# The second weight matrix's scale taken at the first second-product step, and the square of v written into the v tile

## The chip, the cores and the metric

The kernel runs on one core of a Trainium2 chip. Its time is the device time of one execution in microseconds (us); three executions were timed, and their median counts. TensorE (PE) does the matrix products, VectorE (DVE), ScalarE (ACT) and GpSimd (POOL) the rest, and SyncE (SP) starts most of the transfers. Each engine works through its own queue in order.

## The reference, cut to what matters

```python
# attention: B, H, S, D = 4, 8, 576, 64, fp32
scores = causal(q @ k.T / 8 + min(-(cum_i - cum_j), 0))   # cum = cumsum(max(s, 0))
x = softmax(scores) @ v                                    # heads joined: [4, 576, 512]
# first layer
u  = x + real(fft(fft(x, axis=1), axis=2))
un = (u - mean(u)) / sqrt(var(u) + 1e-6)
x  = u + relu(un @ moe_w_ch1) @ moe_w_ch2                  # 512 -> 2048 -> 512
# second layer: the same normalisation (times g_ln) and MLP, without the FFT
```

The weights come as 64-bit floats.

## The kernel before

**Work and stages.** The four batches go through attention, the Fourier layer, a normalisation and the first MLP one after another, in such a way that the MLP of one batch runs beside the attention and the Fourier layer of the next. The second MLP of all batches follows at the end. Attention is worked in pairs of heads, four pairs for a batch: pairs 0 to 3 are batch 0, pairs 4 to 7 batch 1. For these two batches q and k stay in fp32: `prep_pair32` transposes them on TensorE (`tp`, L974 to L985), then come the scores (`s`, L1031), their reduction on VectorE (L1037), the exponentials on ScalarE (L773, L774), a product with the other factor of the decay (`p`, L784), a transpose of `p` by a DMA (`pT`, L788 and L796) and the product with v (`pv`, L818).

**Fourier layer.** `fft_steps` adds and subtracts the two halves of the tokens and of the features into the tiles `eo` (fp16 high and low halves, L1119 and L1120, three tiles for a batch), multiplies by the token matrix (`y`, L1138, 36 products), takes one column apart (`ps`, L1159), and multiplies by the feature matrix (`z`, L1179, 36 products). `emit_ln` normalises the result: `u` (L344, L347), whose tiles a DMA of SP's queue transposes to `unT` (L348).

**Products in two halves.** Except for q and k of batches 0 and 1, each operand of a product is scaled by a power of two and split into a high and a low fp16 half; three products replace one. The scale comes from a norm: squares are summed by ScalarE along with the Square activation, added over the partitions by a small product with ones (`total`, L82, on TensorE) and turned into a power of two by a few operations of one column on VectorE (`pow2_scale`, L93 to L98).

**Weights of the first MLP.** `wa` holds 32 blocks: 0 to 15 of the first matrix, 16 to 31 of the second. `prep` loads each block (512 KB), converts it from 64 bits to fp32 with three VectorE operations (L150, L153, L156; they read the staging tiles `xset` or `wide`), squares it on ScalarE (L167) and splits it on ScalarE (L194) and VectorE (L195). `scale(0)` takes the scale of the first matrix, `scale(1)` that of the second: `wtot` (L171), `total`, and `c2` (L183), by which the second product is multiplied at the end. While `late` is set, the second matrix is split block by block in `emit_g2`, two blocks for each second-product step `m` of batch 0's first chunk.

**MLP.** A chunk is two tiles of 128 tokens; `emit_g1` makes the first product (`g<-unT,wa`, L373) with its rectifier (`h`, L379, L380), and `emit_g2` the second (L395).

**What sets the order.** The kernel is written as generators that are stepped in turn, and a list scheduler then orders the instructions of each engine by a simulated timeline, with priorities. A tile of a pool with `bufs=2` that is asked for a third time waits until the first is free. The square of a pair's v (L991) writes results that nobody reads, into a junk tile of the tag `u16`, which it shares with the `u` tiles and with the weights' squares. The tile for the split v has the tag `v16`.

Of the kernel before, what the change touches and what calls it, by code (L numbers as in the profile page):

```python
# [8 lines left out]
F16 = mybir.dt.float16  # L9
BF16 = mybir.dt.bfloat16  # L10
I32 = mybir.dt.int32
AF = mybir.ActivationFunctionType
# [21 lines left out]
def fused_kernel(ctx: ExitStack, tc, q, k, v, s, wa1, wa2, g_ln, wb1, wb2, tok_c, feat_c, ident_c, rev_c, bias_c, out):  # L34
# [5 lines left out]
    mpool = ctx.enter_context(tc.tile_pool(name="mpool", bufs=2))  # L40
# [7 lines left out]
    att = att_stack.enter_context(tc.tile_pool(name="att", bufs=1))  # L48
# [29 lines left out]
    def total(parts):  # L78

        n = parts.shape[1]  # L80
        ps = ps_s.tile([128, 512], F32, tag="s", name="total")[:, 0:n]
        nc.tensor.matmul(out=ps, lhsT=ones.to_broadcast([128, 128]), rhs=parts, start=True, stop=True)  # L82
        res = small.tile([128, n], F32, tag=f"total{n}", name="total")
        nc.vector.tensor_copy(out=res, in_=ps)
        return res
# [16 lines left out]
    class Weights:  # L102
# [110 lines left out]
        def prep(self):  # L213

            for i in range(len(self.wide + self.extra)):
                self.load(i)
                yield KN["COST"][0]
            held = []
            for i in range(16):
                self.convert(i)  # L220
                self.square(i)
                again = [n for n in range(i + 1, 32) if self.PLACE[n] == self.PLACE[i]]
                if again and self.HOLD and again[0] >= 16:
                    held.append(again[0])
                elif again:
                    self.load(again[0])
                yield KN["COST"][1]
            self.scale(0)
            yield KN["COST"][2]
            left = self.left = list(range(16))  # L230
            for _ in range(KN["S1"] if self.HOLD else KN["S1B"]):
                self.split(left.pop(0))
                yield KN["COST"][3]
            for n, i in enumerate(held):
                self.load(i)
                if n % KN["HOLDN"] == KN["HOLDN"] - 1 or n == len(held) - 1:
                    yield 1.0
            for i in range(16, 32):
                self.convert(i)
                self.square(i)  # L240
                again = [n for n in range(i + 1, 32) if self.PLACE[n] == self.PLACE[i]]
                if again:
                    self.load(again[0])
                yield KN["COST"][1]
                for _ in range(KN["S2"]):
                    if left:
                        self.split(left.pop(0))
                        yield KN["COST"][3]
            while len(left) > (KN["LAZY"] if self.late else 0):
                self.split(left.pop(0))  # L250
                yield KN["COST"][3]
            self.scale(1)
            yield KN["COST"][2]
            for i in range(self.LAST if not self.late else 0):
                self.split(16 + i)
                yield KN["COST"][4]
# [127 lines left out]

    def emit_g2(ch, m, h):
        if m == 0:
            nc.gpsimd.tensor_tensor(out=ch.f, in0=ch.f, in1=ch.w.c2.to_broadcast([128, 2]), op=ALU.mult)
            ch.ps = [ps_2.tile([128, 512], F32, tag=f"g2{j}", name=f"g2{j}") for j in range(2)]
        for i in range(2):
            if ch.w.late:  # L390
                ch.w.split(16 + m + i)
            for j in range(2):
                c = 256 * i + 128 * j
                for n, (lh, lw) in enumerate(((0, 0), (0, 1), (1, 0))):
                    nc.tensor.matmul(  # L395
                        out=ch.ps[j], lhsT=h[:, lh, c:c + 128], rhs=ch.w.w2(lw, m + i),
                        start=(m + i + n == 0), stop=(m + i == MB - 1 and n == 2),
                    )
        if m == MB - 2:
            ch.w.late = False  # L400
            for j in range(2):
                o = mpool.tile([128, 512], F32, tag="o", name="o")
                nc.vector.scalar_tensor_tensor(
                    out=o, in0=ch.ps[j], scalar=ch.f[:, j:j + 1], in1=ch.x[j], op0=ALU.mult, op1=ALU.add
                )
                ch.put(j, o)
# [89 lines left out]
    class MlpStream:  # L496
# [25 lines left out]
        def second(self):  # L522
            ch, m, h = self.pend.pop(0)
            if isinstance(ch.w, Weights7):
                emit_g2x(ch, (m, h))
            else:
                emit_g2(ch, m, h)
# [113 lines left out]
    def prep_pair(p):  # L641

        P = pairs[p]
        b, hp = divmod(p, NPAIR)
        mx = small.tile([128, 3], F32, tag="mx", name="mx")
        for i in range(3):
            nc.scalar.activation(
                out=qk16[:, i].rearrange("p t n -> p (t n)").bitcast(BF16), in_=raw[:, i].rearrange("p t h d -> p (t h d)"), func=AF.Square, accum_out=mx[:, i:i + 1]
            )
        mxa = total(mx)  # L650
        yield
        sc = scs[:, p % 8, :]
        pow2_scale(sc[:, 0:3], sc[:, 3:6], mxa, 15)
        nc.vector.tensor_scalar(
            out=sc[:, 6:7], in0=sc[:, 0:1], scalar1=sc[:, 1:2], scalar2=8.0, op0=ALU.mult, op1=ALU.mult
        )
        nc.vector.tensor_scalar(
            out=sc[:, 7:8], in0=sc[:, 3:4], scalar1=sc[:, 4:5], scalar2=-0.125, op0=ALU.mult, op1=ALU.mult
        )
        P.sc = sc  # L660
        P.ncq = small.tile([128, 5, 2], F32, tag="ncqs", name="ncqs")
        c0 = b * H + 2 * hp
        nc.vector.tensor_scalar(
            out=P.ncq, in0=ncq[:, :, c0:c0 + 2], scalar1=sc[:, 6:7], scalar2=None, op0=ALU.mult
        )
        yield

        for h in range(2):
            hi = qk16[:, h, :, 64 * h:64 * h + 64]
            nc.scalar.activation(out=hi, in_=raw[:, 0, :, h, :], func=AF.Copy, scale=sc[:, 0:1])  # L670
            nc.vector.scalar_tensor_tensor(
                out=qk16[:, h, :, 64 - 64 * h:128 - 64 * h], in0=raw[:, 0, :, h, :], scalar=sc[:, 0:1], in1=hi,
                op0=ALU.mult, op1=ALU.subtract,
            )
        yield
        for h in range(2):
            nc.scalar.activation(
                out=qk16[:, 2 + h].rearrange("p t (r d) -> p t r d", r=2),
                in_=raw[:, 1, :, h:h + 1, :].to_broadcast([128, 5, 2, D]), func=AF.Copy, scale=sc[:, 1:2],
            )  # L680
            nc.vector.scalar_tensor_tensor(
                out=qk16[:, 4, :, 64 * h:64 * h + 64], in0=raw[:, 1, :, h, :], scalar=sc[:, 1:2],
                in1=qk16[:, 2 + h, :, 0:64], op0=ALU.mult, op1=ALU.subtract,
            )
        P.qkT = qkTs[p % 2]
        nc.sync.dma_start_transpose(
            out=P.qkT.rearrange("p b (t n) -> p (b t) n", n=128), in_=qk16.rearrange("p b t n -> p (b t n)")
        )
        yield
        split_v(P, raw[:, 2].rearrange("p t h d -> p t (h d)"))  # L690

    def turn_pair(p):
# [220 lines left out]
            return ps_1.tile([128, 512], F32, tag="g1", name="tp")  # L913
        return ps_2.tile([128, 512], F32, tag=f"g2{i // 2}", name="tp")

    def junk32():

        return mpool.tile([128, 1024], F16, tag="u16", name="junk")[:, 0:640].bitcast(BF16)

    def views32(p):  # L920

        qk = qkTs[p % 2].rearrange("p b n -> p (b n)").bitcast(F32)
        rest = qx.rearrange("p b n -> p (b n)").bitcast(F32)[:, 192 * (p % 2):192 * (p % 2) + 192]
        return qk[:, 0:640], [[(0, 576, qk[:, 640:1216])], [(0, 384, qk[:, 1216:1600]), (384, 576, rest)]]
# [39 lines left out]
    def prep_pair32(p):  # L964

        P = pairs[p]
# [12 lines left out]
        for t in range(4):  # L979
# [7 lines left out]
        put_k(P, ps[:, 64:128], 512, 576)  # L987
        yield
        rv = raw[:, 2].rearrange("p t h d -> p t (h d)")
        mx = small.tile([128, 3], F32, tag="mx", name="mx")  # L990
        nc.scalar.activation(  # L991
            out=junk32(), in_=rv.rearrange("p t n -> p (t n)"), func=AF.Square, accum_out=mx[:, 2:3]
        )
        mxa = total(mx[:, 2:3])
        P.sc = sc = scs[:, p % 8, :]
# [1 line left out]
        yield  # L997
        split_v(P, rv)

    def split_v(P, rv):  # L1000
        P.v = att.tile([128, 5, 2, 128], F16, tag="v16", name="v16", bufs=2)
        nc.scalar.activation(out=P.v[:, :, 0, :], in_=rv, func=AF.Copy, scale=P.sc[:, 2:3])
        nc.vector.scalar_tensor_tensor(
            out=P.v[:, :, 1, :], in0=rv, scalar=P.sc[:, 2:3], in1=P.v[:, :, 0, :], op0=ALU.mult, op1=ALU.subtract
        )
# [482 lines left out]
```

## Time and profile before

| | |
|---|---|
| three executions | 1138.12, 1138.20, 1142.26 us, median 1138.2 |
| profiled execution, its own time | 1139.83 us |
| its span (first to last instruction) | 1138.1 us |
| busy: PE, DVE, ACT, POOL | 994.6, 721.7, 571.8, 603.8 us |
| mean granted clock of TensorE | 0.938 |

The profile is one execution. Times in its rows are microseconds from the start of the span unless marked ns; "x36" counts instructions; what stands in brackets is the time for which the engine had been idle, and what ended that. TensorE is busy 87% of the span, so what a change is worth is read in those stages in which TensorE waits.

### The profile page before, as it was taken

What the parts mean: (1) busy time and instruction counts of PE and PEld (TensorE: products, weight loads), DVE (VectorE), ACT (ScalarE), POOL (GpSimd) and SP (SyncE); (2) the same over time, 40 slices, a digit from 0 to 9 for tenths busy, and PEclk for the clock granted to TensorE, in tenths of its full rate; (3) what the DMA queues carried; (4) which work ended last, traced back from release to release, by engine and by line L of the source; (5) the groups of instructions that cost most, each with busy time, mean ns of one, the idle gap of its engine ahead of it and who ended that gap; (6) DMA issues with size and microseconds to landing.
All of it is one profiled execution on the core that took longest, in us unless ns stands there. A gap on an engine that the chain in (4) does not pass through costs nothing.

```text
span 1138.1 us, 23178 instructions
## 1 busy us (share of the span) xinstructions
PE 994.6 (87%) x8537; PEld 742.3 (65%) x8537; DVE 721.7 (63%) x1720; ACT 571.8 (50%) x1270; POOL 603.8 (53%) x1298
## 2 busy tenths in 40 slices
PE   5667343999999989969999799899999999999998
PEld 3444232766665656535676466566888888888887
DVE  5879977545799855676755697956545434542332
ACT  5678554776477752366722255733333433343332
POOL 3447615787479832497711305347756445645351
PEclk9868675999999989979999899999999999999999
DMA  7989814677459972189830695202111211211000
GB/s 198 262 207 250 216 61 85 142 154 138 99 123 182 187 162 63 31 157 198 141 76 1 195 287 204 65 1 66 29 47 48 51 25 38 56 20 38 20 6 33
DMA packets 286034, 124.17 MB, mean 109 GB/s; under 512 B 267616, under 2 KB 267872, under 8 KB 285920
## 3 DMA queue, kind: packets, MB, share of 16 engines
q1 hardware_dynamic: 285280, 120.59, 46.2%
q0 software_dynamic: 640, 2.10, 0.6%
q8 instruction: 67, 1.10, 0.4%
q14 instruction: 47, 0.39, 0.1%
HBM read 61.50 MB, written 9.51 MB: 62 GB/s over the span
## 4 chain that ended last, share of the span: by engine, by line
PE 50%; DVE 12%; POOL 6%; DMA 5%; issue 3%; ACT 2%; SPq 0%; POOLq 0%; ACTq 0%; DVEq 0%
PE acc L465 14%; PE g L437 8%; PE g1x L437 8%; PE g L373 8%; PE g L395 7%; PE pv L818 1%; PE z L1179 1%; PE y L1138 1%; DMA pT<-p 1%; POOL p L784 1%; DMA wbbig<-in_moe_w_ch_dram 1%; DMA qkT<-qk 1%; PE s L750 1%; DVE h L380 1%; DVE wbbig L156 1%
## 5 line engine op out<-in xcount | busy, mean ns | idle before, releaser
L373 PE MATMUL g<-unT,wa 128*128 128x256 f16 x1728 | 219.3, 279 | 9.6 <-DMA unT<-u 9.6
L395 PE MATMUL g<-wa,h 128*128 128x512 f16 x864 | 208.6, 384 | 7.2 <-DVE h L380 4.5
L373 PEld LDWEIGHTS <-wa 128*128 128x128 f16 x1728 | 168.6, 100 | 51.2 <-issue 12.6
L465 PE MATMUL acc<-wbbig,wa 128*128 128x256 f16 x1512 | 179.4, 274 | 3.7 <-DVE wa L451 2.4
L451 DVE TENSOR_TENSOR wa<-wa,wa 128x896 f16<-128x896 f32 x72 | 78.9, 1096 | 163.6 <-ACT wa L450 163.6
L437 PEld LDWEIGHTS <-wb 128*128 128x128 f16 x1728 | 169.2, 98 | 20.4
L465 PEld LDWEIGHTS <-wa 128*128 128x128 f16 x1512 | 148.3, 98 | 22.5 <-DVE wa L451 2.8
L395 PEld LDWEIGHTS <-h 128*128 128x128 f16 x864 | 82.6, 99 | 93.3 <-DVE h L380 7.3
L450 ACT CAST wa<-wa 128x896 f16<-128x896 f32 x72 | 67.5, 938 | 137.2 <-POOL wa L448 137.2
L773 ACT ACTIVATE p<-sc,mn 128x576 f16<-128x576 f32 (+4 forms) x160 | 90.2, 577 | 69.0 <-DVE mn L751 25.7
L784 POOL TENSOR_TENSOR p<-sc,p 128x129 f16<-128x129 f32 (+4 forms) x104 | 93.3, 900 | 55.3 <-ACT sc L774 54.3
L447 POOL TENSOR_TENSOR wa<-wa 128x128 f32<-128x128 f32 x72 | 49.4, 687 | 109.2 <-ACT wa L444 109.2
L437 PE MATMUL g1x<-unT,wb 128*128 128x256 f16 x864 | 101.8, 273 | 0.0
L818 PE MATMUL pv<-v,pT 128*128 128x64 f16 x1632 | 71.4, 201 | 34.7 <-DVE xset L831 16.8
L437 PE MATMUL g<-unT,wb 128*128 128x256 f16 x864 | 100.9, 273 | 0.0
L818 PEld LDWEIGHTS <-pT 128*128 128x128 f16 x1632 | 64.8, 103 | 50.4 <-issue 31.7
L774 ACT ACTIVATE sc<-sc,mn 128x576 f32<-128x576 f32 (+4 forms) x160 | 91.9, 575 | 1.9
L772 POOL MEMSET p<- 128x128 f16 (+1 forms) x160 | 37.0, 251 | 89.9 <-DMA pT<-p 43.3
L728 POOL TENSOR_TENSOR sc<-cumb,ncqs 128x129 f32<-128x129 f32 (+4 forms) x80 | 66.8, 844 | 19.2 <-DVE cumb L639 14.4
L379 ACT ACTIVATE h<-g 128x512 f16<-128x512 f32 x72 | 42.2, 586 | 53.6 <-PE g L373 53.4
L380 DVE SCALAR_TENSOR_TENSOR h<-g,h 128x512 f16<-128x512 f32 x72 | 49.2, 683 | 30.7 <-ACT h L379 30.5
L1031 PE MATMUL s<-qkT 128*128 128x288 f32 (+4 forms) x192 | 66.9, 444 | 1.4 <-DVE mn L1037 1.4
(244 smaller groups left out, 1710.0 us busy)
## 6 DMA issues: line engine op xcount, KB each, us to landing
wbbig<-in_moe_w_ch_dram SPq DMA_DIRECT2D x32, 512.0 KB
wa<-in_moe_w_ch_dram SPq DMA_DIRECT2D x21, 512.0 KB
cumb<-cumd SPq DMA_DIRECT2D x24, 288.0 KB
xset<-in_moe_w_ch_dram SPq DMA_DIRECT2D x11, 512.0 KB
x2d<-o SPq DMA_DIRECT2D x18, 256.0 KB
raw<-in_v_dram SPq DMA_DIRECT2D x32, 128.0 KB
out_dram<-wa SPq DMA_DIRECT2D x16, 256.0 KB
raw<-in_k_dram SPq DMA_DIRECT2D x24, 128.0 KB
```

What stands on the lines that cost most here:

```text
L373: nc.tensor.matmul(out=ps[:, 256 * i:256 * i + 256], lhsT=ch.w.w1(lw, kk, m + i), rhs=ch.unT[:, 4 * lx + kk, :], start=(n == 0), stop=(n = ...
L395: nc.tensor.matmul(out=ch.ps[j], lhsT=h[:, lh, c:c + 128], rhs=ch.w.w2(lw, m + i), start=(m + i + n == 0), stop=(m + i == MB - 1 and n == 2),)
L437: nc.tensor.matmul(out=ps, lhsT=ch.w.w1(lw, kk, m + 8 * half), rhs=ch.unT[:, 4 * lx + kk, :], start=(n == 0), stop=(n == 11),)
L450: nc.scalar.copy(out=h[:, 0], in_=r[:, 0:7])
L451: nc.vector.tensor_tensor(out=h[:, 1], in0=r[:, 0:7], in1=h[:, 0], op=ALU.subtract)
L465: nc.tensor.matmul(out=acc[key], lhsT=h[:, lh, ia], rhs=b[:, ib, lw], start=(m == 0 and i == 0 and not second), stop=(m == 7 and i == 2 an ...
L728: nc.gpsimd.tensor_tensor(out=u.f[:, 0:n], in0=P.cumb[u.h][:, 0:n], in1=P.ncq[:, t, u.h:u.h + 1].to_broadcast([128, n]), op=ALU.add)
L773: nc.scalar.activation(out=u.w[:, 0:n], in_=u.f[:, 0:n], func=AF.Exp, bias=mn, scale=-1.0)
L774: nc.scalar.activation(out=u.f[:, 0:n], in_=u.f[:, 0:n], func=AF.Exp, bias=mn, scale=-1.0, accum_out=u.rs[:, h:h + 1])
L784: eng.tensor_tensor(out=u.w[:, w:w + n], in0=u.f[:, 0:n], in1=u.w[:, 0:n], op=ALU.subtract)
L818: nc.tensor.matmul(out=ps[:, c], lhsT=pT[:, lp * nb + kb, :], rhs=P.v[:, kb, lv, c], start=(n == 0), stop=(n == 3 * nb - 1),)
L1031: nc.tensor.matmul(out=ps[:, b - a:e - a], lhsT=P.qT[:, o:o + 128], rhs=kt[:, b - k0:e - k0], start=not pe, stop=not pe or (not masked and ...
```

## The change

Two edits. `scale(1)` of `wa` is no longer a step of `prep`; while `late` is set it is called in `emit_g2` at the first second-product step, and the splits of the second matrix, which need its result, follow it. The square of a pair's v in attention 0 and 1 writes its unread results into the high half of the v tile that the split fills afterwards, so that this tile is asked for one step earlier and the junk tile is gone.

```diff
@@ prep
-            self.scale(1)
+            if not self.late:
+                self.scale(1)
             yield KN["COST"][2]
@@ emit_g2
         if m == 0:
+            if ch.w.late:
+                ch.w.scale(1)
             nc.gpsimd.tensor_tensor(out=ch.f, in0=ch.f, in1=ch.w.c2.to_broadcast([128, 2]), op=ALU.mult)
@@ prep_pair (batches 2, 3)
         yield
+        P.v = v_tile()
         split_v(P, raw[:, 2].rearrange("p t h d -> p t (h d)"))
@@ attention of batches 0, 1
-    def junk32():
-
-        return mpool.tile([128, 1024], F16, tag="u16", name="junk")[:, 0:640].bitcast(BF16)
@@ prep_pair32
+        P.v = v_tile()
         mx = small.tile([128, 3], F32, tag="mx", name="mx")
         nc.scalar.activation(
-            out=junk32(), in_=rv.rearrange("p t n -> p (t n)"), func=AF.Square, accum_out=mx[:, 2:3]
+            out=P.v[:, :, 0, :].bitcast(BF16), in_=rv, func=AF.Square, accum_out=mx[:, 2:3]
         )
@@ split_v
+    def v_tile():
+        return att.tile([128, 5, 2, 128], F16, tag="v16", name="v16", bufs=2)
+
     def split_v(P, rv):
-        P.v = att.tile([128, 5, 2, 128], F16, tag="v16", name="v16", bufs=2)
```

The scheduler draws the whole order anew. On TensorE, at the end of attention 0, this stood before (`wtot` is the sum for the second matrix, `eo_1742` the first of batch 0's three eo tiles, `v_1227` the v of attention 0's last pair):

```order
L818 LDWEIGHTS pT
L818 MATMUL pv<-v_1227,pT 128x64
L82 MATMUL total<-wtot,ones 128x1
L1138 LDWEIGHTS eo_1742
L1138 MATMUL y<-tok,eo_1742 128x320
```

In the changed kernel the total of `wtot` is not there; six y products of the first eo tile stand ahead of the last eighteen pv of attention 0, and the other thirty y products behind them. The total now stands on TensorE behind batch 0's z, the transposes of pair 4, the total of its v square (`mx`) and the first scores of attention 1:

```order
L974 MATMUL tp<-ident,raw 128x128 x4
L980 MATMUL tp<-ident,raw 128x128 x4
L984 MATMUL tp<-ident,raw 128x64
L985 MATMUL tp<-ident,raw 128x64
L82 MATMUL total<-mx,ones 128x1
L1034 MATMUL s<-qkT_104 128x129 x2
L1034 MATMUL s<-qkT_104 128x288 x3
L1034 MATMUL s<-qkT_104 128x96
L1034 MATMUL s<-qx,qkT_104 128x192
L82 MATMUL total<-wtot,ones 128x1
L822 LDWEIGHTS pT
L822 MATMUL pv<-v_2046,pT 128x64
```

Behind these rows come the rest of twelve pv of pair 4 (`v_2046`), the transposes of pair 5 with further scores, and then the first g of batch 0; before, g stood ahead of the pv and of pair 5's transposes.

On ScalarE, the square of pair 4's v stood before between the u tiles of the first chunk (`u_1969`, `u_1975`) and those of the second:

```order
L194 ACTIVATE wa_193<-spare,wasc 128x512 x2
L344 ACTIVATE u_1969<-xset_107,va 128x512
L344 ACTIVATE u_1975<-xset_107,va 128x512
L991 ACTIVATE junk,mx<-raw 128x640
L344 ACTIVATE u_2223<-xset_107,va 128x512
```

In the changed kernel it stands ahead of the last two eo tiles of batch 0:

```order
L1118 COPY eo<-xm_204 64x2
L1118 COPY eo<-xe 128x2
L167 ACTIVATE junk,wafro<-wa_192 128x512
L992 ACTIVATE v_2046,mx<-raw 128x5x128
L1122 ACTIVATE eo_1766<-eo,fs 128x512
L1122 ACTIVATE eo_1778<-eo,fs 64x512
```

It has moved past the whole Fourier layer, and the second halves of the weights' splits (L194) have left the place ahead of the u tiles.

In SP's queue, after the bias loads of attention 1 (`cumb`), the transposes of u came first before (`u_1969` and `u_1975` are the two halves of the first chunk):

```order
L634 DMA cumb<-cumd 128x576 x2
L348 DMA_TRANSPOSE unT<-u_1969 128x8x128
L348 DMA_TRANSPOSE unT<-u_1975 128x8x128
L348 DMA_TRANSPOSE unT<-u_2223 128x8x128
L947 DMA raw<-in_v_dram 128x4x64 x2
L950 DMA raw<-in_v_dram 64x2x64
L796 DMA_TRANSPOSE pT<-p_2112 128x8x128
```

In the changed kernel (`u_1954` and `u_1960` are the same two halves) they stand behind the first pT transpose of attention 1, the v loads of pair 5 and a q load of pair 7, which goes into the tile `qk` that pair 5's transposes on TensorE read:

```order
L637 DMA cumb<-cumd 128x576 x2
L800 DMA_TRANSPOSE pT<-p_2096 128x8x128
L947 DMA raw<-in_v_dram 128x4x64 x2
L950 DMA raw<-in_v_dram 64x2x64
L940 DMA qk_102<-in_q_dram 128x2x64
L349 DMA_TRANSPOSE unT<-u_1954 128x8x128
L941 DMA qk_102<-in_q_dram 128x2x64
L349 DMA_TRANSPOSE unT<-u_1960 128x8x128
```

Five transfers of attention 1 have moved ahead of the first transpose of u, and a sixth between the two.

## Rows read from the trace of the kernel before

**Rows 1.** Windows: start:end length, busy of PE, PEld, DVE, ACT, POOL; clock, DMA share
```profile
139.82:154.90 15.08, 0.00 (x0) 0.00 (x0) 11.36 (x22) 5.14 (x13) 4.99 (x8) 0.50 0.45 126
154.90:167.71 12.81, 12.80 (x101) 8.61 (x101) 9.96 (x24) 9.57 (x19) 0.83 (x5) 0.87 0.01 3
167.71:191.01 23.30, 2.88 (x16) 2.44 (x17) 19.30 (x49) 10.89 (x24) 13.68 (x41) 0.59 0.32 74
167.71:186.70 18.99, 1.43 (x10) 1.05 (x10) 17.96 (x45) 9.25 (x21) 10.50 (x23) 0.61 0.25 63
191.01:215.00 23.99, 23.99 (x178) 17.24 (x177) 14.05 (x48) 17.59 (x42) 13.02 (x25) 0.90 0.61 119
480.00:500.00 20.00, 8.04 (x54) 3.45 (x54) 18.43 (x58) 14.44 (x32) 17.25 (x42) 0.65 0.69 145
```

**Rows 2.** Timeline of TensorE: start, duration, instructions, in brackets the idle time before
```profile
33.90 0.58 PE L82 MATMUL total<-mx,ones 128*128 128x1 f32 x2 [3.46 <-ACT junk L991]
...
154.90 0.59 PE L82 MATMUL total<-wtot,ones 128*128 128x1 f32 x2 [15.08 <-DVE wtot L171]
155.35 6.94 PE L1138 MATMUL y<-tok,eo 128*128 128x320 f16 x36
...
163.47 4.24 PE L1179 MATMUL z<-feat,yT 128*128 128x257 f16 x36
...
189.56 0.59 PE L82 MATMUL total<-mx,ones 128*128 128x1 f32 x2 [18.22 <-ACT junk L991]
190.01 1.21 PE L1031 MATMUL s<-qkT 128*128 128x129 f32 x4
191.01 5.09 PE L373 MATMUL g<-unT,wa 128*128 128x256 f16 x24
...
204.46 0.51 PE L818 MATMUL pv<-v,pT 128*128 128x64 f16 x12
```

**Rows 3.** Timeline of VectorE, the same columns
```profile
145.43 1.40 DVE L1120 SCALAR_TENSOR_TENSOR eo<-eo,fs,eo 64x512 f16<-64x512 f32 x2
...
186.01 0.69 DVE L347 TENSOR_TENSOR u<-un,u 128x512 f16<-128x512 f32 x1
...
193.14 0.91 DVE L1003 SCALAR_TENSOR_TENSOR v<-raw,scs,v 128x640 f16<-128x640 f32 x1 [0.93 <-ACT v L1002]
```

**Rows 4.** Timeline of ScalarE, the v square of pair 4
```profile
188.68 0.74 ACT L991 ACTIVATE junk<-raw 128x640 bf16<-128x640 f32 x1 [3.50 <-issue]
```

**Rows 5.** Windows of line L195 alone: VectorE busy; clock, DMA share, GB/s
```profile
154.90:167.71 12.81, 7.28 (x10) 0.87 0.01 3
167.71:186.70 18.99, 5.37 (x6) 0.61 0.25 63
```

**Rows 6.** Window of line L1037 alone: VectorE busy
```profile
191.00:201.00 10.00, 2.46 (x12) 0.76 0.47 84
```

**Rows 7.** Timeline of SP's queue
```profile
169.53 0.47 SPq L940 DMA_DIRECT2D raw<-in_q_dram  x1
...
175.53 5.54 SPq L634 DMA_DIRECT2D cumb<-cumd  x2
```

**Rows 8.** Window of line L1031 alone: PE, PEld busy
```profile
191.00:208.00 17.00, 3.75 (x16) 2.21 (x15) 0.86 0.59 112
```

**Rows 9.** Window of tile tp alone: PE, PEld, DVE, ACT busy
```profile
203.00:208.00 5.00, 1.54 (x10) 1.14 (x10) 0.42 (x1) 1.71 (x5) 1.00 0.92 186
```

**Rows 10.** Lines L195 and L194: count, ns min/median/max, first and last start
```profile
L195 DVE SCALAR_TENSOR_TENSOR wa<-wa,wasc,wa x30: 732/746/1598, 81.4 to 178.0; 128x512 f16<-128x512 f32 x30
...
L194 ACT ACTIVATE wa<-wa,wasc x30: 704/721/747, 80.7 to 174.5; 128x512 f16<-128x512 f32 x30
```

**Rows 11.** Waits of SP's queue: line <- releaser: us in total, times, longest
```profile
SPq L348 <- PE g1x L437: 146.8, 7, 22.8
...
SPq L940 <- PE tp L974: 19.8, 1, 19.8
```

## The prediction

> **What bounds the kernel now.** I read the windows by stage first, since the share of busy time says nothing about a single stall. The stretch from 191.01 us on, where batch 0's first MLP runs beside attention 1, has TensorE busy for 23.99 of 23.99 us; ahead of it lie 23.30 us with 2.88 busy and 15.08 us with none [rows 1]. TensorE's timeline then names what ends these two holes [rows 2]: the first ends at 154.90 in a total, two tiny matmuls that had waited 15.08 us for wtot, the summed squares of the second weight matrix; the second ends at 189.56 in another total that had waited 18.22 us for the v square of pair 4. Between the two stand y and z, the Fourier products of batch 0, and behind the second come the first score products s and then g, the first MLP product. VectorE's timeline says when the work could have gone on [rows 3]: y needs the last eo tiles, written by 145.43 + 1.40 = 146.83, while y began at 155.35; g needs unT, the transpose of two u tiles of which the second is written by 186.01 + 0.69 = 186.70, while g began at 191.01. So the 15.08 us hole is partly the weight total's fault, and the 18.22 us one is only nominally the square's: ended earlier it would not let g start, since u comes at 186.70 whatever TensorE does.
>
> **The change part by part.** The order fences show where the scheduler now puts things.
>
> 1. The weight total leaves y's path. It stands behind y, z, the transposes of pair 4 and the first s, so the last y may begin at 146.9. Six of y's 36 products, those of the first eo tile, now stand ahead of the last 18 pv, in time that was idle: 6 x 6.94/36 = 1.2 us less behind the last eo [rows 2]. z ended at 163.47 + 4.24 = 167.71; now it ends at 167.71 - (155.35 - 146.9) - 1.2 = 158.1, which is 9.6 us earlier. Bounds: the v square of pair 4 now stands on ScalarE ahead of the last two eo activations, at 0.74 us as before [rows 4], so y may lose 0 to 0.74; I take 0, since ScalarE is busy 5.14 of the 15.08 us there [rows 1].
>
> 2. From z to the second u. Before, these are 186.70 - 167.71 = 18.99 us, and VectorE is busy 17.96 of them, so it sets their length [rows 1]. What leaves it are six second halves of w2 splits, 5.37 us [rows 5]. What comes in is attention 1's start, which stood behind the u tiles: the twelve reductions of the first units, 2.46 us [rows 6], the second half of pair 4's v split, 0.91 [rows 3], and small operations of the two totals and the first normalisation of some 0.15 to 0.34 each, which I put at 2 us together: 5.4. That is a wash. The second u is then written at 158.1 + 19.0 = 177.1. Bounds: 5.4 earlier, if none of the added ones gets in front in time, and 5.4 later, if the freed time had been idle anyway.
>
> 3. From the second u to g: 191.01 - 186.70 = 4.31 us for the transposes. In SP's queue a q load of pair 7 now stands between them, 0.47 [rows 7]: g starts at 177.1 + 4.3 + 0.5 = 181.9, which is 9.1 us earlier. The queue ahead must be empty by then: the cumb loads, begun at 175.53 and 5.54 long in the queue, should begin as much earlier as z ends, so end at 171.5 [rows 7], and the first unit's pT transpose, the raw v loads and the q load have until 177.1. That is close.
>
> 4. Work pulled in front of g. The stretch from 191.01 holds the s products of the first units (16, 3.75 us) [rows 8], the ten transposes of pair 5 (1.54) [rows 9] and the first twelve pv (0.51) [rows 2]. These now run before the first g, in what was a hole: 5.8 us. As TensorE idles nowhere in the old stretch, they count in full, provided that the other engines keep up.
>
> 5. At nothing: the v squares are the same instruction with another output tile. In attention 0 the totals of the squares also held TensorE, once for 3.46 us [rows 2]; that gain is 0 to 3.5 and I take 0, because the weight conversions on VectorE, and not TensorE, set the end of attention 0. The sixteen splits of w2 that ran between 154.90 and 186.70 now run two per second-product step beside the MLP: 0.721 each on ScalarE and 0.746 on VectorE [rows 10], hidden by the stretch's slack of 6.4 and 9.9 us [rows 1]; sixteen are 11.5 and 11.9 us, so the cover holds only if they spread over more than that stretch.
>
> Sum: 9.1 + 5.8 = 14.9 us. The profiled execution took 1139.83 us with a span of 1138.1; it is 1.63 above the median of 1138.2. The span should come to 1123.2, such an execution to 1124.9 and the median to **1123.3 us**.
>
> **The rivals.** *More is won later.* Between 480 and 500 us TensorE is busy 8.04 of 20.00 us [rows 1], for want of products that are ready. In the new order 22 fewer g products of L373 stand ahead of the end of batch 2's z (720 against 742), so that many are left to fill that hole: 24 of them take 5.09 us [rows 2], 22 take 4.7, and the time is 1118.6. Against it: with the whole order redrawn, such filler could as well be missing elsewhere.
>
> *ScalarE becomes the bound.* If all sixteen first halves fall into the stretch after the first g, its 17.59 us become 29.1 in 24.0 [rows 1, 10]; the 5.1 over come off the gain: 1128.4.
>
> *The splits run slow beside GpSimd.* One L195 took 1.598 us where the median is 0.746 [rows 10], and before, six took 5.37 us beside a GpSimd busy 10.50 of 18.99 us while ten took 7.28 beside one busy 0.83 of 12.81 [rows 1, 5]: 0.90 against 0.73 each. The new place has GpSimd busy 13.02 of 23.99. With all sixteen at 1.598, VectorE has 14.05 + 16 x 1.598 = 39.6 us of work in 24.0, 15.6 over: the gain is gone, 1138.2 - 14.9 + 15.6 = 1138.9. It decides when h and v splits, which wait on VectorE, hold TensorE. The Trainium skill, "SBUF — State Buffer", section "Who interferes with whom", says that a VectorE instruction with two inputs in SBUF contends with a GpSimd one that reads SBUF. By that rule the moved splits pay, and the trace agrees in direction, with 0.90 against 0.73 us.
>
> *SP's queue holds g back.* The transposes of u now stand behind a pT transpose and a q load that must wait for TensorE's transposes of pair 5, which stand behind the first pv. This load waited 19.8 us for them once, and the transposes of u have waited up to 22.8 us for TensorE [rows 11]. Behind these waits stands everything that g needs. If the queue stands still for 22.8 us past 177.1, the gain of 14.9 turns into a loss of 7.9: 1146.1. It is slower than before from a hold of 14.9 us on, and measurably from 20.6. For it speaks that the slack in part 3 is small; against it, that the old wait had a long run of other products ahead of it on TensorE, and the new one has only s and twelve pv.
>
> **How the numbers follow.** A difference of 0.5%, 5.7 us, is about what a measurement of this kernel can tell from none. Chances: the forecast (1123.3) 0.42, more won later (1118.6) 0.16, ScalarE (1128.4) 0.14, slow splits (1138.9) 0.17, SP's queue (1146.1) 0.11. The first three are faster by over 0.5% (0.72), the fourth is the same (0.17), the last slower (0.11). For 8 in 10 the first three and about half of the fourth must be inside: 1113 (the second's time less the 5.4 that part 2 could add) to 1140. The likeliest alone goes from 1118, with part 2's gain, to 1129, with its loss.
>
> **What would show it.** Right: y's last products start near 147 on TensorE, z ends near 158, the weight total waits under 1 us, and the first g starts near 182 with s, ten transposes and twelve pv before it. Wrong: y still begins past 150 (another input is late); u is written past 180 though z ended early (part 2); SP's queue waits at L940 while u lies ready; VectorE or ScalarE busy for all of the first 24 us behind g, with TensorE idle behind h, or L195 above 1 us there; or stalls that are longer in the later stages, where the redrawn order has nothing to do with the two edits.

## The result

The changed kernel takes 1127.28 us (median of five, 1122.61 to 1128.89), the kernel before 1138.2 (five, 1135.36 to 1142.26): a ratio of 0.9881, 95% interval 0.9857 to 0.9906. Forecast were 1123.3 us within 1113 to 1140, and faster with 0.72. The profiled execution took 1122.61 us with a span of 1120.7; it is the fastest of its five, which matters below. By the medians the change wins 10.9 us here and 13.5 in a second comparison (1126.3 against 1139.81 us, below), where 14.9 had been forecast.

**Profile after.** TensorE's timeline, to be held against [rows 2]:

```profile
133.77 1.78 PE L1141 MATMUL y<-tok,eo 128*128 128x320 f16 x6 [2.52 <-ACT eo L1122]
135.35 1.17 PE L822 MATMUL pv<-v,pT 128*128 128x64 f16 x18
...
141.15 3.49 PE L1141 MATMUL y<-tok,eo 128*128 128x320 f16 x12 [0.66 <-DVE eo L1123]
146.35 2.67 PE L1141 MATMUL y<-tok,eo 128*128 128x320 f16 x9 [1.71 <-DVE yT L1146]
...
152.50 3.91 PE L1182 MATMUL z<-feat,yT 128*128 128x255 f16 x27
...
169.84 0.28 PE L82 MATMUL total<-wtot,ones 128*128 128x1 f32 x2
172.33 0.82 PE L822 MATMUL pv<-v,pT 128*128 128x64 f16 x12 [2.21 <-DMA pT<-p]
...
179.70 7.78 PE L374 MATMUL g<-unT,wa 128*128 128x256 f16 x48 [1.64 <-DMA unT<-u]
```

The weight total waits for nothing now. z ends at 152.50 + 3.91 = 156.41 (forecast 158.1, before 167.71), the first g starts at 179.70 (forecast 181.9, before 191.01), with scores, transposes and twelve pv ahead of it. VectorE's timeline, against [rows 3], has the last eo and the second u:

```profile
140.35 1.54 DVE L1123 SCALAR_TENSOR_TENSOR eo<-eo,fs,eo 128x512 f16<-128x512 f32 x2
...
174.61 0.69 DVE L348 TENSOR_TENSOR u<-un,u 128x512 f16<-128x512 f32 x1
```

The second u is written at 175.30 (forecast 177.1). The last eo was written at 141.89, 4.9 us sooner than before, which the forecast had left where it was. The stretches of the program follow, all engines, with the columns of [rows 1]: from z of batch 0 to g, from g to the end of batch 1's z, to batch 2's, to batch 3's, to the end. Before (the first of these stretches is the third row of [rows 1]):

```profile
191.01:318.89 127.88, 121.59 (x1110) 87.06 (x1109) 75.41 (x247) 81.34 (x204) 83.66 (x182) 0.98 0.63 127
318.89:467.79 148.90, 142.92 (x1248) 90.64 (x1248) 109.43 (x302) 82.85 (x197) 90.80 (x209) 0.98 0.69 135
467.79:617.13 149.34, 134.12 (x1186) 85.33 (x1187) 97.65 (x280) 79.79 (x189) 87.92 (x201) 0.93 0.60 115
617.13:1138.10 520.97, 496.55 (x4170) 408.89 (x4170) 283.65 (x503) 209.05 (x390) 248.63 (x520) 0.99 0.23 67
```

After:

```profile
156.41:179.70 23.29, 12.65 (x54) 8.68 (x55) 21.84 (x75) 15.52 (x40) 15.61 (x43) 0.67 0.54 110
179.70:306.32 126.62, 116.38 (x1067) 83.21 (x1067) 82.02 (x239) 83.14 (x202) 86.95 (x183) 0.97 0.60 123
306.32:453.53 147.21, 142.35 (x1232) 89.16 (x1232) 110.13 (x301) 82.38 (x195) 89.99 (x208) 0.98 0.68 136
453.53:599.78 146.25, 136.53 (x1208) 87.28 (x1209) 99.55 (x280) 79.75 (x189) 88.00 (x201) 0.96 0.60 118
599.78:1120.70 520.92, 497.22 (x4171) 409.60 (x4170) 283.41 (x503) 208.15 (x390) 250.85 (x520) 0.98 0.23 67
```

So 11.3 us are won up to z of batch 0, nothing from there to g, 1.3 from g to batch 1's z, where 5.8 had been forecast, 1.7 in the next stretch, 3.1 in the one behind it, and nothing in the tail. The counts of TensorE's instructions (x1110, x1067) are what makes stretches comparable: an order that moves products over a boundary changes a stretch's length without a gain. In the well-filled third stretch of before a matmul costs 142.92 / 1248 = 0.115 us.

### The profile page after: what moved, and what is told of

Read it like the earlier page. It is cut to its first block, busy times and chain, and to the rows that moved or that the text cites. A ratio compares the mean times of both kernels' runs of the same rounds, so it can differ in the third digit from the quotient of the medians.

```text
span 1120.7 us, 23179 instructions
## 1 busy us (share of the span) xinstructions
PE 1005.1 (90%) x8537; PEld 746.0 (67%) x8537; DVE 722.8 (64%) x1720; ACT 569.6 (51%) x1270; POOL 608.7 (54%) x1298
## 4 chain that ended last, share of the span: by engine, by line
PE 55%; DVE 18%; POOL 7%; DMA 6%; issue 3%; ACT 3%; SPq 1%; POOLq 0%; DVEq 0%; ACTq 0%
PE acc L468 14%; PE g L374 9%; PE g L440 8%; PE g L398 8%; PE g1x L440 8%; DMA pT<-p 3%; PE pv L822 2%; POOL p L788 2%; PE y L1141 1%; PE z L1182 1%; PE s L1034 1%; DVE h L381 1%; PE s L754 1%; POOL sc L732 1%; DVE st L325 1%
## 5 line engine op out<-in xcount | busy, mean ns | idle before, releaser
L374 PE MATMUL g<-unT,wa 128*128 128x256 f16 x1728 | 223.4, 281 | 10.5 <-DMA unT<-u 10.5
L450 POOL TENSOR_TENSOR wa<-wa 128x128 f32<-128x128 f32 x72 | 51.8, 720 | 108.1 <-ACT wa L447 108.1
L732 POOL TENSOR_TENSOR sc<-cumb,ncqs 128x129 f32<-128x129 f32 (+4 forms) x80 | 68.3, 862 | 22.4 <-DVE cumb L642 14.9
L1034 PE MATMUL s<-qkT 128*128 128x288 f32 (+4 forms) x192 | 71.4, 468 | 5.5 <-DVE mn L1040 3.0
```

The costliest lines, as they stand in the source:

```text
L374: nc.tensor.matmul(out=ps[:, 256 * i:256 * i + 256], lhsT=ch.w.w1(lw, kk, m + i), rhs=ch.unT[:, 4 * lx + kk, :], start=(n == 0), stop=(n = ...
L732: nc.gpsimd.tensor_tensor(out=u.f[:, 0:n], in0=P.cumb[u.h][:, 0:n], in1=P.ncq[:, t, u.h:u.h + 1].to_broadcast([128, n]), op=ALU.add)
L1034: nc.tensor.matmul(out=ps[:, b - a:e - a], lhsT=P.qT[:, o:o + 128], rhs=kt[:, b - k0:e - k0], start=not pe, stop=not pe or (not masked and ...
```

## The experiments

All ratios are to the kernel before, run beside each on the same chip; stretches are named as above.

**Scale alone.** Only the first two hunks of the change.

```diff
-            self.scale(1)
+            if not self.late:
+                self.scale(1)
...
+            if ch.w.late:
+                ch.w.scale(1)
```

> Only the scale of the second matrix is moved; the square of v keeps its junk tile. Theory (the terms add up as forecast): y no longer waits for the weight total, z of batch 0 ends near 156.5 as in the changed kernel instead of 167.7. In this order no score products, transposes or pv of attention 1 beyond pair 4's first two stand ahead of the first g, and the six w2 splits have left the stretch between z and u without anything in their place, so u comes some 5 us sooner after z and g starts near 175, 16 us earlier than before; the stretch from g to the end of batch 1's z stays as long as before (127.9). Time 1119 to 1125, about that of both edits together. Rival (the square of v carries the gain, since its total was the wait of 18.2 us): g starts later than 183, time 1130 or more. Rival (the redrawn order of the later stages carries it): the stretches behind batch 1's z shrink by more than the 11 us that are won ahead of it.

1134.69 us, ratio 0.9951 (0.9929 to 0.9973). z ended at 163.96, not 156.5: the last eo came at 147.05 as before, and z took long (last section). The stretch to g is 18.23 us against 23.30, so the w2 splits were worth 5 us there, as forecast. But the next one grew from 127.88 to 134.16 with the same work:

```profile
163.96:182.19 18.23, 3.53 (x16) 3.09 (x17) 14.56 (x41) 6.22 (x15) 12.18 (x38) 0.59 0.39 94
182.19:316.35 134.16, 122.42 (x1112) 87.52 (x1111) 89.12 (x270) 92.45 (x222) 87.24 (x186) 0.97 0.61 121
```

TensorE idles 11.7 us in it, before 6.3. The two stretches together are 152.4 us, before 151.2: what the splits gave back ahead of g they took behind it. My theory, by which this edit carried nearly the whole gain, fell.

**Square alone.** Only the other hunks.

```diff
-            out=junk32(), in_=rv.rearrange("p t n -> p (t n)"), func=AF.Square, accum_out=mx[:, 2:3]
+            out=P.v[:, :, 0, :].bitcast(BF16), in_=rv, func=AF.Square, accum_out=mx[:, 2:3]
```

> Only the square of v is moved into the v tile; the scale stays in prep. Theory: TensorE still waits some 15 us for the weight total ahead of y, less what attention 0 wins by its squares no longer waiting (0 to 4 us); z ends at 164 to 168. The w2 splits and attention 1's start now both stand between z and the second u, which makes that stretch some 5 us longer (24 us), g starts near 192 to 197; scores, ten transposes and 27 pv, some 7.5 us, are done before g. Ends 1130 to 1137. Rival (the square carries the gain): time below 1128, as with both edits, with g at 183 or earlier. Rival (attention 0 alone won, by the squares' buffer): the end of attention 0's pv moves from 139.8 to about 136 to 138 and nothing else changes, 1134 to 1136.

1129.63 us, ratio 0.9909 (0.9889 to 0.9929), just below the 1130 to 1137 that was expected. TensorE's timeline:

```profile
133.00 1.12 PE L819 MATMUL pv<-v,pT 128*128 128x64 f16 x18 [2.62 <-DVE xset L832]
151.15 0.59 PE L82 MATMUL total<-wtot,ones 128*128 128x1 f32 x2 [17.04 <-DVE wtot L171]
151.60 5.42 PE L1138 MATMUL y<-tok,eo 128*128 128x320 f16 x27
```

Attention 0 ends at 134.1, before at 139.8, and the last eo is written at 140.14 + 0.88 = 141.02; the weight total then eats the gain, and z ends at 164.48. The two stretches behind it are 28.72 and 114.49 us:

```profile
164.48:193.20 28.72, 16.26 (x70) 9.98 (x70) 24.50 (x76) 19.25 (x48) 17.31 (x43) 0.56 0.53 104
193.20:307.69 114.49, 109.70 (x1029) 78.67 (x1029) 69.18 (x218) 71.52 (x177) 80.23 (x180) 0.99 0.62 131
```

Here 81 products fewer are left behind g, and the stretch is 13.4 us shorter: work pulled ahead of g does count in full where no splits take its place. From z to z the two are 143.2 us against 151.2; 27 of TensorE's instructions fewer (1099 against 1126) are 3.1 of the difference, so 4.9 are won. Eleven of the sixteen L195 ran here before z ended, beside y and z.

**The changed kernel, and the kernel before, once more.**

> The changed kernel unaltered, for a second profile beside the others on one chip. Theory: its profiled execution was the fastest of five (1122.6 against 1126.8 to 1128.9) because attention 0, which is paced by weight loads, ended early: in an execution near 1127 the last eo is written 3 to 5 us later than 141.9, and the stretches from z of batch 0 on keep their lengths within 1 us. Rival: the lengths from z on differ, by 4 us in all, in a later stage (the stretches with transposes in SP's queue), and the start is the same.

> The kernel before unaltered, for a second profile. Theory: the end of y, z and the first g lie within 3 us of the first profile's, and the stretches between z of batch 0 and the end of batch 3's z within 1 us. Rival: a stretch behind z of batch 0 differs by 3 us or more, and the comparison of stretches between the two kernels would be no finer than that.

The changed kernel: 1126.3 us, ratio 0.9869 (0.9848 to 0.9891), profiled span 1124.9. z ended at 156.65; the stretches are 24.34, 126.07, 147.12, 149.28 and 521.44 us. So of the 4.2 us between the two profiles 3.0 lie in the stretch to batch 3's z and 1.1 between z and g; its rows from g to the end of batch 1's z and to batch 3's are

```profile
180.99:307.06 126.07, 116.82 (x1067) 83.32 (x1067) 80.45 (x237) 82.19 (x197) 85.66 (x180) 0.97 0.61 123
...
454.18:603.46 149.28, 138.25 (x1208) 87.81 (x1209) 100.37 (x280) 79.52 (x189) 87.81 (x201) 0.95 0.59 115
```

The last eo came at 141.36, against 141.89; the theory of an early attention 0 was wrong. The kernel before repeated itself within 0.3 us in every stretch (span 1138.7). By these two second profiles the gain is 10.9 up to z, -1.1 to g, then 1.9, 1.9, 0.3 and -0.2: 13.8 us.

**Junk in another scratch tile.** The kernel before with one line changed.

```diff
-        return mpool.tile([128, 1024], F16, tag="u16", name="junk")[:, 0:640].bitcast(BF16)
+        return mpool.tile([128, 512], F32, tag="un", name="un", bufs=1).bitcast(BF16)[:, 0:640]
```

> The kernel before with one edit: the square of v writes its junk into the tile of un (the normalisation's scratch) in place of the tag it shares with the squares of the weights; neither the v tile nor the scale is touched. Theory (the square edit shortens attention 0 only because it takes v's squares out of the turn of the weights' squares, whose tiles wait for weight loads): the last eo is written near 141 as with the square edit alone, not at 146.8; the weight total still holds TensorE, z ends near 164.5; the pair-4 square, which must now take turns with un, stays late, so few scores stand ahead of g and the stretch from g to batch 1's z is 122 to 128. Time 1133 to 1136. Rival (the v tile itself matters, asked for one step earlier): eo at 146 to 147, z at 167 to 168, time as before.

1136.78 us, ratio 0.9966 (0.9945 to 0.9986). The profiled execution took 1143.17 us and is the slowest of twelve.

```profile
130.90 1.12 PE L818 MATMUL pv<-v,pT 128*128 128x64 f16 x18 [2.02 <-DVE xset L831]
154.76 0.59 PE L82 MATMUL total<-wtot,ones 128*128 128x1 f32 x2 [22.74 <-DVE wtot L171]
155.21 9.79 PE L1138 MATMUL y<-tok,eo 128*128 128x320 f16 x36
166.17 4.24 PE L1179 MATMUL z<-feat,yT 128*128 128x257 f16 x36
```

Attention 0 ends at 132.0 and the last eo at 139.07 (138.34 + 0.73), 7.8 us sooner than before, without the v tile: what held it was the tag that v's squares shared with the weights' squares, and the rival is out. In this profile none of it arrives, since the total waits until 154.76 for the last weight blocks as before. That part of the theory missed: z ended at 170.41 and not near 164.5, in part because y ran long (last section). Up to z the edits need each other: the scale alone wins 3.8 us, the square alone 3.2, both 11.3. The whole times do not say so: by the medians of one chip the scale alone wins 5.1 us, the square alone 10.2, both 13.5, so the square alone brings most of the gain.

**Without the low halves of the late splits.**

```diff
             nc.scalar.activation(out=dst[:, 0:512], in_=self.raw(i), func=AF.Copy, scale=sc)
+            if i >= 16 and self.late:
+                return
...
         def w2(self, lo, m):
+            if self.pre == "wa":
+                lo = 0
```

> The changed kernel with the second halves (L195) of the sixteen late w2 splits left out; the products read the high half twice, so this part of the computation is changed and its amount on TensorE is not. The order of all engines else is the same. Theory (the moved splits cost the stretch behind the first g some 4 us, because VectorE has them in front of the reductions and h): the stretch from the first g to the end of batch 1's z falls from 126.3 to 121 to 123, the idle time of TensorE in it from 9.7 to some 5 to 6, the time to 1121 to 1124. Rival (ScalarE's first halves or the waits for transposes cost it): it stays above 125, time 1126 to 1127.

1123.77 us, ratio 0.9852 (0.9825 to 0.9878).

```profile
181.61:305.79 124.18, 117.90 (x1067) 84.42 (x1067) 66.80 (x221) 81.38 (x197) 81.62 (x180) 0.96 0.66 125
```

TensorE idles 6.3 us, as the theory had it, against 9.3 and 10.2 in the two profiles of the changed kernel; but its busy time is 1.1 to 1.5 higher for the same products, and the stretch is only 1.9 to 2.4 us shorter, half of what was expected. By these profiles (one of this run, two of the changed kernel) VectorE's halves of the splits cost the stretch some 2 us; the whole time shows no more, since the interval overlaps that of the changed kernel (0.9848 to 0.9891). ScalarE's halves were not taken away (L194 is ScalarE's first half of a split, L195 VectorE's second).

The two traces show something else. These are the first 24 us behind g, all engines, and GpSimd's time for three operations of attention 1 in them (busy us, mean ns of one; then the idle time before), first in the changed kernel, then without the low halves:

```profile
179.70:203.70 24.00, 23.28 (x196) 16.88 (x196) 20.97 (x45) 19.10 (x45) 21.08 (x41) 0.90 0.59 125
L732 POOL TENSOR_TENSOR sc<-cumb,ncq 128x448 f32<-128x448 f32 x2 | 2.4, 1180 | 0.1
L732 POOL TENSOR_TENSOR sc<-cumb,ncq 128x320 f32<-128x320 f32 x2 | 2.1, 1034 | 0.1
L788 POOL TENSOR_TENSOR p<-sc,p 128x320 f16<-128x320 f32 x2 | 2.0, 1015 | 0.0
...
181.61:205.61 24.00, 24.00 (x206) 17.86 (x206) 10.04 (x37) 19.70 (x44) 16.32 (x39) 0.91 0.58 122
L736 POOL TENSOR_TENSOR sc<-cumb,ncq 128x448 f32<-128x448 f32 x2 | 1.8, 932 | 0.1
L736 POOL TENSOR_TENSOR sc<-cumb,ncq 128x320 f32<-128x320 f32 x2 | 1.4, 720 | 0.0
L792 POOL TENSOR_TENSOR p<-sc,p 128x320 f16<-128x320 f32 x2 | 1.6, 793 | 0.0
```

These three take 1.27 to 1.44 times as long beside the splits (others, such as `sc` of 128x257, the same 0.61 us), so what the splits cost may be GpSimd's time as well as VectorE's; no run separates the two. Nor is it paid where the splits stand: TensorE idles only 0.72 of these 24 us in the changed kernel, and its longest wait in the stretch, 2.99 us for `xm`, VectorE's scaling of a product pv, ends at 239.46, 31 us after the last split.

**Last tile first.**

```diff
-                for i in range(3):
+                for i in (2, 1, 0):
                     r = rows[i]
                     for le, lt in ((0, 0), (0, 1), (1, 0)):
```

> The changed kernel, but each y sum begins with the last eo tile, so that all 36 y products stand behind the last eo and run in one piece. Theory (the short waits inside y leave TensorE's granted clock low, and z pays for it: 7.4 to 7.8 us against 5.42): y starts near 142 and z takes under 6.5 us at a clock above 0.8, its end is at 154.5 to 156 although six y fewer are done early. Rival (z is slow because TensorE had been idle, whatever y's shape): z again 7.3 us or more at 0.7 or less and ends at 157 to 158. The later stages are redrawn in this order; the whole time 1122 to 1131.

1123.07 us, ratio 0.9841 (0.9814 to 0.9868): 3 us below the changed kernel, but the intervals overlap. z ended at 159.20, later than either theory had it, and took 6.97 us: y still paused for 2.39 us, for a copy of its results as in the changed kernel, so a y in one piece was not tested. What was won stands behind z: from z to z it is 146.1 us with 1117 instructions, in the changed kernel 149.9 and 150.4 with 1121 and 1122. The windows around the pause (TensorE busy; clock) show what it did:

```profile
145.20:146.20 1.00, 1.00 (x6) 0.54 1.12 209
146.20:147.20 1.00, 0.97 (x7) 1.00 0.97 334
147.20:149.50 2.30, 0.00 (x0) 1.00 0.21 80
149.50:150.50 1.00, 0.94 (x4) 0.52 0.00 0
150.50:151.50 1.00, 1.00 (x6) 0.50 0.00 0
151.50:152.50 1.00, 1.00 (x13) 0.50 0.00 0
152.50:153.50 1.00, 1.00 (x14) 0.50 0.00 0
153.50:154.50 1.00, 1.00 (x7) 0.50 0.00 0
154.50:155.50 1.00, 1.00 (x12) 0.50 0.00 0
155.50:156.50 1.00, 1.00 (x8) 0.57 0.00 0
156.50:157.50 1.00, 1.00 (x12) 1.00 0.03 8
```

**Scale after the first normalisation.** The call stands behind the loop over the first `emit_ln`, not in `emit_g2`.

```diff
-            if ch.w.late:
-                ch.w.scale(1)
...
+        wa.scale(1)
         attns = {1: gated(urgent((attn_steps32 if N32 > 1 else attn_steps)(1), KN["A1OFF"]), wa.mark)}
```

> Both edits, but the scale of the second matrix is taken right after the first normalisation is written, and not at the first second-product step: the total stands on TensorE right behind batch 0's z, and the w2 splits are again ready ahead of the first g. Theory (the terms add): z ends at 156.5 as in the changed kernel; the stretch to g is 27 to 29 us, as with the square edit alone, since splits and attention 1's start both lie in it; the stretch from g to the end of batch 1's z is 114 to 117, since scores, transposes and pv are done and no split is left in it; by batch 1's z some 5 to 7 us are won over the changed kernel. Time 1118 to 1123. Rival (VectorE's work has to be done before batch 1's z wherever it stands): the two stretches together stay near 150, time 1126.

1126.04 us, ratio 0.9876 (0.9850 to 0.9902), no better than the change. z ended at 157.06; the two stretches are 26.07 and 121.70 us, 147.8 in all with 1104 instructions on TensorE, where the changed kernel has 149.9 with 1121: 17 x 0.115 = 2.0 of the 2.1 us are work moved on. That speaks for the rival, but only five of the sixteen L195 stand ahead of g here (3.71 us) and eleven behind it (9.89 us), so the run does not show that all of them would cost the same on either side.

**Both variants.**

> The two variants together: each y sum begins with the last eo tile, and the scale of the second matrix is taken right after the first normalisation. Theory as the runs so far have it (from z of batch 0 to z of batch 1 VectorE's splits cost what the early scores give, so their place within it moves the first g but not the end): z of batch 0 ends at 158 to 160, the first g stands later than 190 since even more scores and pv are ahead of it, the stretch from z to z is 146 to 149 as in either variant, and the time is 1121 to 1125, as with the last tile first alone. Rival (the two gains of 3 us and of 2 us add): the stretch from z to z falls to 143 or less, 1117 to 1120.

1124.52 us, ratio 0.9876 (0.9852 to 0.9901), z at 158.27, g at 188.95 (a little under what was expected), from z to z 147.7. The gains do not add. No version measured is shown to beat the changed kernel.

## Why the prediction was right, point by point

**Part 1, up to z (9.6 us forecast, 11.3 and 10.9 measured).** The total left y's path and y no longer waited for it. But the size came out of two errors of opposite sign. "I take 0" for the bound on attention 0's squares was wrong: the last eo came 4.9 us sooner, since v's squares no longer take turns with the weights' squares (the scratch-tile run shows the tag alone does that). And "the last y may begin at 146.9" at the old pace of y and z was wrong too: from the last eo to the end of z it took 14.5 us, where 5.8 + 5.4 = 11.2 had been reckoned. Before, y ran in one piece behind the long wait and z at full clock; now y has pauses, and for most of its time z ran at half the clock (0.67 on average, last section).

**Part 2, z to u, a wash: right.** 18.9 us (156.41 to 175.30) against 18.99. Two experiments show the sum's halves near their price of 5.4: the same length is 13.86 us with neither splits nor scores in it (scale alone), 5.1 less, and 25.16 with the scores beside the last five splits (square alone), 6.2 more.

**Part 3, u to g: right.** 4.4 us, where 4.8 had been forecast; in the second profile it was 5.4.

**Part 4, the pulled work (5.8 us): the work was sized rightly, and it was paid back.** The stretch behind g has 43 TensorE instructions fewer and 5.2 us less busy time, but idles 10.2 us instead of 6.3, so 1.3 to 1.9 us are left. The step that failed is part 5's, that the sixteen moved splits are hidden by the stretch's slack. Ten of them stood before beside y and z, where VectorE had little else to do (7.28 of its 9.96 us), and six ahead of g; now most stand behind g, between reductions and h. The slack itself was there: in the first 24 us behind g VectorE is busy 20.97 us, ScalarE 19.10, and TensorE idles 0.72. The idle time comes later, in waits of attention 1, which a sum of busy times leaves out; that GpSimd, slowed beside the splits, hands it on is likely and not shown. With no pulled work the same move costs 6.3 us behind g (scale alone), with no moved splits the pulled work counts in full (square alone).

**The rivals.** *ScalarE* and *the slow splits* were priced at 5.1 and 15.6; some 4 us of such a cost came, of which VectorE's halves account for 2 by one profile; how much is ScalarE's stays open. In the first 24 us behind g thirteen L195 took 11.49 us:

```profile
179.70:203.70 24.00, 11.49 (x13) 0.90 0.59 125
```

That is 0.88 each, about the 0.90 of [rows 5] beside a busy GpSimd and far from 1.598. The Trainium skill, "SBUF — State Buffer", section "Who interferes with whom", says that a VectorE instruction with two inputs in SBUF contends with a GpSimd one that reads SBUF. The trace agrees in direction (0.88 beside GpSimd busy 21.08 of 24.00 us, 0.73 beside one nearly idle), and so does the run without the low halves, for GpSimd; no run here shows that the port is the cause. *SP's queue* did not hold g: the q load waited for TensorE's transposes until 173.67, and the second u came at 175.30.

*More is won later* came true beside the forecast. In the stretch to batch 3's z the changed kernel runs 22 instructions more in 3.1 and 0.3 us less (first and second profile). The other orders say the same: 66 more for 3.1 us (scale alone), 53 more for 2.2 (square alone), 69 more for 3.2 (last tile first), where 0.115 each would be 7.6, 6.1 and 7.9. Products left over do fill the holes there, and the fill was worth 2.9 to 5.6 us. The stretch to batch 2's z, 1.7 us shorter with 16 instructions fewer (1.8 us), won nothing itself; it only handed them on. Why the two profiles of the change differ by 3.0 us in the stretch to batch 3's z, with equal counts, stays open.

The sum, then, with the second profiles: 10.9 up to z, 1.1 lost to g, 1.9 behind g, and 2.0 later, 13.8 us where 14.9 had been forecast. That the total came so near was in part luck: part 1 was made of two errors of opposite sign, and a gain that had been put among the rivals stood in for about half of the 3.9 us that were paid back. The forecast also laid the gain at the weight total's door; by whole times the square alone brings 10.2 us and the scale alone 5.1.

## What to carry to other kernels

When work is moved off a waiting engine's path, ask which idle time it used to stand in: ten splits stood free beside y and z, where TensorE was busy 12.80 of 12.81 us, and behind g, where all engines are busy, the moved splits cost 2 to 6 us. Two edits that each end a different wait for the same start (here the eo tiles and the weight total) are worth little alone up to that start; what each is worth to the whole kernel only its own run shows. Compare stages by length and by count of products together; an order drawn anew moves products over every boundary.

## What was not expected of the hardware

For the products behind it, one long wait can cost less than several short ones. From the end of y to the end of z (with the small products `ps`) it took 5.42 us at a granted clock of 1.00 (2.4 GHz) in the kernel before, where y had run without a pause; 7.39 us at 0.67 on average in the changed kernel; and with the scale alone, behind pauses of 5.28 and 1.91 us in y, 10.17 us at 0.50 (1.2 GHz). In this order:

```profile
162.29:167.71 5.42, 5.42 (x64) 4.57 (x63) 3.92 (x10) 3.94 (x9) 0.83 (x5) 1.00 0.00 2
...
149.02:156.41 7.39, 7.39 (x63) 5.47 (x63) 2.49 (x8) 2.55 (x8) 0.83 (x5) 0.67 0.00 1
...
153.79:163.96 10.17, 9.74 (x64) 6.72 (x65) 2.38 (x11) 3.28 (x9) 0.91 (x5) 0.50 0.00 1
```

With the last tile first the clock had just risen to 1.00 when y paused for 2.3 us; it came back at 0.52 and stayed low for some 6 us of unbroken products (the windows above). But a long wait is no assurance: behind an idle time of 22.7 us, with the junk in another tile, y needed 9.79 us for the same 36 products, at 0.50 until 164, that took 6.94 behind 15.1 us and 6.91 behind 17.0 (square alone): y alone lost 2.9 us there. The length of the wait alone does not order these three; what does stays open. The Trainium skill, "TensorE: Matmul & The Clock Gate", section "Part 1: The HAM clock gate (the "warmup" mystery)", describes a clock that idling lowers and activity raises. The rows agree on the two levels and on the direction; how soon the clock came back differed from run to run.
